# Outputs read 512 bytes at a time and K and V read 32 KB at a time in a grouped-query attention kernel

## The chip, the cores and the metric

The kernel runs on one core of a Trainium2 chip. The metric is the device time of one execution in microseconds (us), and lower is better. Differences between two kernels are judged on runs of both on the same chip.

## What is computed

Grouped-query attention with a softmax over all keys, in bfloat16. There are 16 batches, 32 query heads, 8 key/value heads, 16 query positions, 2048 key positions and a head size of 128.

```python
def reference(q, k, v):                     # q (16, 32, 16, 128), k and v (16, 8, 2048, 128)
    rep = Hq // Hkv                         # 4 query heads share one head of K and V
    k = jnp.repeat(k, rep, axis=1)
    v = jnp.repeat(v, rep, axis=1)
    scores = jnp.einsum("bhqd,bhkd->bhqk", q, k) * D ** -0.5
    p = _softmax(scores, axis=-1)
    return jnp.einsum("bhqk,bhkd->bhqd", p, v)
```

One (batch, key/value head) has 2048 x 128 values of K, 512 KB, as much of V, and 4 x 16 = 64 rows of queries. K and V together are 134.2 MB (millions of bytes), queries and outputs 2.1 MB each.

## The kernel before

**Pairs.** The 128 (batch, head) groups are worked on two at a time: 64 pairs, `NP`. The two groups' 64 query rows fill the 128 partitions. A pair needs one K tile and one V tile of 1 MB each (128 partitions of 8 KB) and makes one output tile of 128 rows of 256 bytes, 32 KB.

**The stages of a pair.** VectorE transposes the K tile in 32x32 blocks (L474). TensorE makes the scores in PSUM (L345). VectorE scales them into SBUF and takes each row's minimum (L494). GpSimd exchanges these between the two halves of the partitions (L216 to L224). ScalarE takes the exponentials (L542). TensorE transposes the probabilities (L363), ScalarE evicts them to SBUF (L553), and four pairs later (`PVLAG`) TensorE multiplies them with V (L415). ScalarE scales the product by the reciprocal row sum into an output tile (`norm`, L566). Every fourth pair a 128 KB tile of queries is spread and transposed for the next four pairs.

**Loads.** SyncE (SP) issues all K and V loads in one fixed order, K six pairs ahead of V (`VLAG`). K has `NK` = 8 buffers, and the load into a buffer waits until the transpose of its last tenant is done (L273). V has `NV` = 4 buffers, and a load waits until the product of the pair four before is done (L285). The helper `load` (L169) writes the descriptors' shape out by hand: the read side of a K or V tile is 64 runs of 16 KB, which are contiguous in DRAM, and the write side is 128 rows of 8 KB, so each run read is written into two partitions. The first two K tiles are ordinary copies of 128 rows of 8 KB (L276). The V tiles of the last eight pairs (from `P4` = 56) are loaded a head at a time, in reads of 8 KB that are written as two rows of 4 KB.

**Stores.** The outputs of the first `PH` = 48 pairs are stored one pair at a time by ScalarE's own DMA queue (`store`, L570): 128 reads of 256 bytes from SBUF, 128 writes of 256 bytes to DRAM. There are `NO` = 8 output buffers `Osb`, each with a semaphore `sem_o`; `norm` waits on it before it writes a buffer again. In a step, ScalarE runs `exp`, every second pair of four `queries`, `norm` of the pair four before, `evict`, and then issues that pair's store. The outputs of pairs 48 to 62 stay in the tile `Oh` and are stored at the end by SP (L300), and the last pair has a store of its own.

**Loops.** `steps` (L121) unrolls the first four steps, runs steps 4 to 51 in a hardware loop whose body has eight steps, and unrolls the rest. In the loop the pair's number is a register.

Of the kernel before, what the change touches and what calls it, by code (L numbers as in the profile page):

```python
# [12 lines left out]
NV = 4  # L13
NKT = 2
NPT = 4
NO = 8
NQ = 2
NR = 8
VLAG = 6
PVLAG = 4  # L20
# [5 lines left out]
def bass_standalone__gqa_softmax__sampling_kernel(  # L26
# [3 lines left out]
    v: bass.AP,  # L30
    out: bass.AP,
):

# [32 lines left out]
    Sneg = [sb(f"Sneg{i}", [128, Sk], F32) for i in range(2)]  # L68
    P = [sb(f"P{i}", [128, Sk // 2], F32) for i in range(2)]
    PT = [sb(f"PT{i}", [128, 8, 128], F32) for i in range(NPT)]  # L70
    Osb = [sb(f"O{i}", [128, 128], BF16) for i in range(NO)]
    Oh = sb("Oh", [128, sum(HELD), 128], BF16)

    own = sb("own", [128, NR, 4], F32)
# [43 lines left out]
    assert (HI - LO) % LOOP == 0 and HI <= P4 - 2  # L118


    def steps(eng, step, end):  # L121
        for p in range(LO):
            step(p, p)
        with eng.Fori(LO, HI, LOOP) as base:
            for i in range(LOOP):
                step(base + i, LO + i)
        for p in range(HI, end):
            step(p, p)


    def v_tile(p):
        return Kn[p % 4 + (NP - 8) % NK] if p >= NP - 4 else Vb[p % NV]

    def out_tile(p, i):
        return Oh[:, p - PH, :] if isinstance(p, int) and PH <= p < NP - 1 else Osb[i % NO][:, :]

    def stage_ap(u):
        return ST_ps[:, 512 * u:512 * (u + 1)]
# [27 lines left out]
        eng.dma_start(Qn[s][:, :, :].rearrange("a j d -> a (j d)"), src).then_inc(sem_q[s], 16)  # L166


    def load(eng, dst, src, x, n):  # L169
        ap = lambda t, dims: eng.lower_ap_dma(bass.AP(t.tensor, t.offset, dims))  # L170
        return eng.add_instruction(mybir.InstDMACopy(  # L171
            name=nc.get_next_instruction_name(), engine=eng.engine, mode="Copy", queue="qSPDynamicHW",
            ins=ap(src, [[n * x, 128 // n], [1, 1], [1, n * x]]), outs=ap(dst, [dst.ap[0], [1, 1], [1, x]])))

    lo, hi = slice(0, 64), slice(64, 128)

    with nc.Block() as block:
# [90 lines left out]
        @block.sync  # L268
        def _(sp):
            def load_k(p):  # L270
                s = p % NK
                if p >= NK:
                    sp.wait_ge(sem_kt, p - NK + 1)  # L273
                src = kf[128 * p:128 * (p + 1), :]
                if p < 2:
                    ins = sp.dma_start(Kn[s][:, :], src)  # L276
                else:
                    ins = load(sp, Kn[s][:, :], src, 4096, 2)
                ins.then_inc(sem_k[s], 16)

            def load_v(p):
                if p >= NP - 4:
                    sp.wait_ge(sem_kt, p - 3)
                elif p >= NV:
                    sp.wait_ge(sem_pv, p - NV + 1)  # L285
                dst = v_tile(p)[:, :]
                done = sem_vx[p - NP + 4] if NP - 4 <= p < NP - 1 else sem_v[p % NV]
                if p < P4:
                    load(sp, dst, vf[128 * p:128 * (p + 1), :], 4096, 2).then_inc(done, 16)
                    return  # L290
                dst = dst.rearrange("a (g x) -> a g x", g=2)
                src = vf4[:, 2 * p:2 * p + 2, :]
                if p < NP - 1:
                    for h in range(2):
                        load(sp, dst[:, h, :], src[:, h, :], 2048, 2).then_inc(done, 16)
                    return
                for n, x in enumerate((slice(0, 1536), slice(1536, 2048))):
                    sp.dma_start(dst[:, :, x], src[:, :, x]).then_inc(sem_vl[n], 16)

            def store_held(p, n):  # L300
                sp.wait_ge(sem_nm, p + n + 1)
                dst = of[128 * p:128 * (p + n), :].rearrange("(x r) d -> r x d", x=n)
                sp.dma_start(dst, Oh[:, p - PH:p - PH + n, :]).then_inc(sem_oh, 16)

            load_q(sp, 0, 0)
            for t in range(NP + VLAG):
                if t < NP:
                    load_k(t)
                for c in range(2, NQC):
                    if t == 4 * c - QLEAD:  # L310
                        if c == NQ:
                            sp.wait_ge(sem_q4d, 2)
                        sp.wait_ge(sem_q4, max(2, 4 * c - 6))
                        load(sp, Qn[c % NQ][:, :, :], qf[512 * c:512 * (c + 1), :], 512, 2).then_inc(sem_q[c % NQ], 16)
                if 0 <= t - VLAG < NP:
                    load_v(t - VLAG)
            p = PH
            for n in HELD:
                store_held(p, n)
                p += n  # L320
            sp.wait_ge(sem_oh, 16 * len(HELD))
            for s in range(NO):
                sp.wait_ge(sem_o[s], 16 * (PH // NO + 1 + (s == NO - 1)))

        @block.tensor
        def _(pe):
# [185 lines left out]
        @block.scalar  # L512
        def _(act):
            act.wait_ge(sem_id, 1)
            act.activation(warm[:, 1:2], warm[:, 0:1], ACT.Exp).then_inc(sem_nm, 1)

            with act.Fori(1, 2, 1) as c:
                load_q(act, c, 1)

            for s in range(NO):  # L520
                act.nop(nofuse=True).then_inc(sem_o[s], 16)


            def queries(c, b, base=0):
                act.wait_ge(sem_tq, base + 4 * c + 2 * b + 2)
                if c >= 2 and b == 0:
                    act.wait_ge(sem_qs, base + 4 * (c - 1))
                act.activation(  # L528
                    QT[c % 2][:, b, :].rearrange("p (a j) -> p a j", j=4),
                    q_stage_ap(c, b).rearrange("p (j a) -> p a j", j=4), ACT.Copy,  # L530
                ).then_inc(sem_evq, 2)

            def exp(p, i):
                act.wait_ge(sem_b, p + 1)
                if i >= 2:
                    act.wait_ge(sem_st[1], p - 1)
                order = "p (h t x) -> p h t x" if isinstance(p, int) and p >= P4 else "p (t h x) -> p h t x"
                to = P[i % 2][:, :].bitcast(BF16).rearrange(order, x=128, h=2)
                of_s = Sneg[i % 2][:, :].rearrange(order, x=128, h=2)
                s, t = i % NR, (i + 1) % NR  # L540
                for h in range(2):
                    ins = act.activation(  # L542
                        to[:, h], of_s[:, h], ACT.Exp,
                        bias=nbias[:, s, h:h + 1], scale=-1.0, accum_out=own[:, t, 2 + h:3 + h],
                    )
                ins.then_inc(sem_exp, 1)

            def evict(p, i):
                for h in range(2):
                    act.wait_ge(sem_st[h], p + 1)  # L550
                    if h == 0 and i >= NPT:
                        act.wait_ge(sem_pv, p - NPT + 1)
                    act.activation(  # L553
                        PT[i % NPT][:, 4 * h:4 * (h + 1), :].rearrange("p t q -> p (t q)"),
                        p_stage_ap(p, h), ACT.Copy,
                    ).then_inc(sem_ev[h], 1)

            def norm(p, i):
                s = i % NR
                act.wait_ge(sem_pv, p + 1)  # L560
                act.wait_ge(sem_rec, p + 1)
                if not isinstance(p, int) or p < PH:
                    act.wait_ge(sem_o[i % NO], 2 * (p - i) + 16 * (i // NO + 1))
                elif p == NP - 1:
                    act.wait_ge(sem_o[i % NO], 16 * (PH // NO + 1))
                act.activation(  # L566
                    out_tile(p, i), o_ap(p), ACT.Copy, scale=rrec[:, s:s + 1],
                ).then_inc(sem_nm, 1)

            def store(p, i):  # L570
                act.wait_ge(sem_nm, p + 2)
                rows = bass.ds(128 * p, 128)
                act.dma_start(of[rows, :], Osb[i % NO][:, :]).then_inc(sem_o[i % NO], 16)

            def step(p, i):
                exp(p, i)
                if i % 4 < 2 and (not isinstance(p, int) or p + 4 < NP):
                    queries(i // 4 + 1, i % 4, p - i)
                if i >= PVLAG:
                    norm(p - PVLAG, i - PVLAG)  # L580
                evict(p, i)
                if i >= PVLAG and (not isinstance(p, int) or p < PH + PVLAG):
                    store(p - PVLAG, i - PVLAG)

            for b in range(2):
                queries(0, b)
            steps(act, step, NP - 3)
            exp(NP - 3, NP - 3)
            norm(NP - 7, NP - 7)
            exp(NP - 2, NP - 2)  # L590
            evict(NP - 3, NP - 3)
            norm(NP - 6, NP - 6)
            exp(NP - 1, NP - 1)
            evict(NP - 2, NP - 2)
            norm(NP - 5, NP - 5)
            evict(NP - 1, NP - 1)
            for p in range(NP - 4, NP):
                norm(p, p)
            store(NP - 1, NP - 1)


# [26 lines left out]
```

## Time and profile before

| what | value |
|---|---|
| median of 3 runs | 335.8 us (335.75 to 336.75) |
| the profiled execution's own time | 335.8 us |
| its span, first to last instruction | 333.9 us |
| VectorE busy | 294.8 us, 88% |
| TensorE busy | 279.1 us, 84% |
| ScalarE busy | 258.8 us, 78% |
| GpSimd busy | 149.4 us, 45% |
| moved by DMA | 138.61 MB in 21854 packets, 415 GB/s over the span |

The profile counts the packets of the 16 DMA engines by what is read: one packet is one run that a transfer reads, and every transfer has 16 packets of 4 bytes besides, one for each engine, which count up its semaphore. The share of a queue is the time that its packets took, summed, divided by 16 times the length of the stretch. The queue q1 is SP's and q10 is ScalarE's.

### The profile page before, as it was taken

Reading aid. Unit: us, or ns where it says so; the run is one execution under the profiler, and the core shown is the slowest. Engines: PE = TensorE matmul, PEld = TensorE weight load, DVE = VectorE, ACT = ScalarE, POOL = GpSimd, SP = SyncE. Lnnn points to the kernel's source line nnn. Section 1 sums busy time; section 2 is a strip of 40 time slices with the busy share of each in tenths; the row PEclk is TensorE's granted clock in tenths of the full one; section 3 lists DMA queues with packets and bytes.
Section 4 is the critical chain, followed back from the end, with each engine's and each line's share of the span. In section 5 each row is a group of like instructions: output and inputs, shape, how many; then the busy total and the mean of one; then the engine's idle time right before and its main releaser. Section 6 shows DMA issues by size and latency. Waiting matters only on the chain.

```text
span 333.9 us, 16112 instructions
## 1 busy us (share of the span) xinstructions
PE 279.1 (84%) x6542; PEld 209.1 (63%) x6542; DVE 294.8 (88%) x354; ACT 258.8 (78%) x482; POOL 149.4 (45%) x488
## 2 busy tenths in 40 slices
PE   2557979999998989888897988979879798788786
PEld 1234757777776766666665766757657567667464
DVE  3999998999999989989898898998999989999930
ACT  3286887989897979779688787887878787886873
POOL 4444455353645544354445435354363453543330
PEclk9996999999999999999999999999999999999999
DMA  8999999999999999999999999999999999999997
GB/s 316 422 412 432 413 412 426 418 425 422 426 422 431 427 422 425 423 422 425 420 426 421 424 422 426 430 417 428 421 425 422 426 420 418 426 422 413 409 408 261
DMA packets 21854, 138.61 MB, mean 415 GB/s; under 512 B 11472, under 2 KB 11984, under 8 KB 13136
## 3 DMA queue, kind: packets, MB, share of 16 engines
q1 hardware_dynamic: 14640, 136.69, 97.7%
q10 hardware_dynamic: 7200, 1.74, 2.4%
q8 instruction: 8, 0.13, 0.2%
q14 instruction: 6, 0.05, 0.0%
HBM read 136.31 MB, written 2.10 MB: 415 GB/s over the span
## 4 chain that ended last, share of the span: by engine, by line
DMA 57%; PE 17%; DVE 16%; issue 7%; ACT 1%; SPq 1%; POOL 1%; DVEq 0%; POOLq 0%
DMA Vb<-in_v_dram 44%; PE O_ps L415 10%; DVE KT L474 9%; DMA Kn<-in_k_dram 8%; DVE Sneg L494 7%; DMA Kn<-in_v_dram 5%; PE ST_ps L363 3%; PE S_ps L345 3%; ACT P L542 1%; SPq L171 1%; PE ST_ps L378 1%; PE ST_ps L404 0%; POOL nbias L224 0%; SPq L276 0%; SPq L166 0%
## 5 line engine op out<-in xcount | busy, mean ns | idle before, releaser
L474 DVE STREAM_TRANSPOSE KT<-Kn 128x2048 f32<-128x2048 f32 x64 | 147.7, 2308 | 21.0 <-DMA Kn<-in_k_dram 20.9
L542 ACT ACTIVATE P<-Sneg,nbias 128x1024 bf16<-128x1024 f32 x128 | 146.0, 1142 | 15.1 <-POOL nbias L224 13.2
L494 DVE TENSOR_SCALAR_CACHE_REDUCE Sneg<-S_ps 128x1024 f32<-128x1024 f32 x128 | 149.9, 1206 | 3.0 <-PE S_ps L345 2.8
L415 PE MATMUL O_ps<-Vb,PT 64*64 64x128 bf16 x3584 | 111.1, 216 | 30.9 <-issue 26.8
L415 PEld LDWEIGHTS O_ps<-Vb,PT 64*64 64x64 bf16 x3584 | 102.9, 107 | 49.9 <-issue 49.9
L553 ACT ACTIVATE PT<-ST_ps 128x512 f32<-128x512 f32 x126 | 68.5, 594 | 15.7 <-PE ST_ps L363 15.0
L345 PE MATMUL S_ps<-KT,Qs 32*64 32x512 bf16 x2048 | 74.3, 399 | 6.0 <-DVE Sneg L494 3.9
L363 PE MATMUL ST_ps<-ident,P 128*128 128x128 f32 x504 | 69.7, 282 | 8.3 <-ACT P L542 8.3
L216 POOL COPY oth<-own 64x4 f32<-64x4 f32 (+1 forms) x65 | 11.9, 183 | 136.4 <-DVE Sneg L494 134.3
L363 PEld LDWEIGHTS ST_ps<-ident,P 128*128 128x128 f32 x504 | 54.7, 142 | 16.6 <-ACT P L542 10.9
L345 PEld LDWEIGHTS S_ps<-KT,Qs 32*64 32x64 bf16 x2048 | 27.6, 106 | 30.5 <-issue 17.1
L198 POOL COPY Qs<-QT 128x512 bf16<-128x512 bf16 x64 | 39.0, 610 | 12.1 <-POOL rowsum L231 6.0
L224 POOL TENSOR_SCALAR nbias<-own,oth 128x1 f32<-128x1 f32 x128 | 33.9, 280 | 10.6 <-POOL oth L219 9.0
L566 ACT ACTIVATE O<-O_ps,rrec 128x128 bf16<-128x128 f32 x48 | 17.5, 365 | 26.6 <-PE O_ps L415 26.5
L161 POOL COPY Q<-Qn 128x1024 bf16<-128x1024 bf16 x31 | 32.4, 1044 | 1.3 <-DMA Qn<-in_q_dram 1.3
L231 POOL TENSOR_TENSOR rowsum<-own,oth 64x1 f32<-64x1 f32 x128 | 23.8, 186 | 8.2
L378 PEld LDWEIGHTS ST_ps<-ident,Q 128*128 128x128 f32 x128 | 14.4, 148 | 18.3 <-issue 18.3
L378 PE MATMUL ST_ps<-ident,Q 128*128 128x128 f32 x128 | 22.1, 300 | 4.5 <-POOL Q L161 4.5
L542 ACT ACTIVATION_READ_ACCUMULATOR P<-Sneg,nbias 128x1 f32 x128 | 24.1, 188 | 0.0
L528 ACT ACTIVATE QT<-ST_ps 128x512 f32<-128x512 f32 x32 | 18.5, 578 | 3.7 <-PE ST_ps L378 3.7
L219 POOL COPY oth<-own 64x4 f32<-64x4 f32 (+1 forms) x65 | 11.8, 181 | 7.3
L566 ACT ACTIVATE Oh<-O_ps,rrec 128x128 bf16<-128x128 f32 x12 | 4.4, 367 | 9.6 <-PE O_ps L415 6.7
(30 smaller groups left out, 44.6 us busy)
## 6 DMA issues: line engine op xcount, KB each, us to landing
Kn<-in_k_dram SPq DMA_DIRECT2D x64, 1024.0 KB, 20.2
Vb<-in_v_dram SPq DMA_DIRECT2D x56, 1024.0 KB, 18.3
Vb<-in_v_dram SPq DMA_DIRECT2D x8, 512.0 KB, 15.6
Kn<-in_v_dram SPq DMA_DIRECT2D x6, 512.0 KB, 14.7
Qn<-in_q_dram SPq DMA_DIRECT2D x15, 128.0 KB, 20.0
out_dram<-O ACTq DMA_DIRECT2D x49, 32.0 KB, 8.9
Kn<-in_v_dram SPq DMA_DIRECT2D x1, 768.0 KB, 17.7
out_dram<-Oh SPq DMA_DIRECT2D x3, 128.0 KB, 15.8
```

Of the source, the lines that this page charges most:

```text
L161: return eng.tensor_copy(Q4[:, :, b, :, :], src.unsqueeze(2).to_broadcast([128, 4, 4, 64]))
L198: gp.tensor_copy(Qs[i % 2][:, :, :], QT[i // 4 % 2][:, :, 128 * x:128 * (x + 1)].bitcast(BF16)).then_inc(sem_qs, 1)
L224: ins = gp.tensor_scalar(nbias[:, s, h:h + 1], own[:, s, h:h + 1], oth[:, s, h:h + 1], None, op0=ALU.min)
L231: gp.tensor_tensor(rowsum[rows, t:t + 1], own[rows, s, 2 + h:3 + h], oth[rows, s, 2 + h:3 + h], op=ALU.add,).then_inc(sem_sum[h], 1)
L345: ins = pe.matmul(S_ps[64 * w:64 * (w + 1), 512 * r:512 * (r + 1)], qs[rows, b, f, 64 * h:64 * (h + 1)], kt[rows, w, b, f], start=(acc == ...
L363: ins = pe.transpose(dst[:, 128 * t:128 * (t + 1)], P[i % 2][:, 128 * x:128 * (x + 1)], ident4[:, :])
L378: ins = pe.transpose(dst[:, 128 * j:128 * (j + 1)], src[:, j, b, :], ident4[:, :])
L415: ins = pe.matmul(out[rows, :], pt[rows, w, t, e, :], vt[rows, x, :], start=(x == 0), stop=(x == 31),)
L474: ins = dve.transpose(dst, src)
L494: ins = dve.tensor_scalar(dst, src, -scale, None, op0=ALU.mult, op1=ALU.min, accum_out=own[:, i % NR, h:h + 1],)
L542: ins = act.activation(to[:, h], of_s[:, h], ACT.Exp, bias=nbias[:, s, h:h + 1], scale=-1.0, accum_out=own[:, t, 2 + h:3 + h],)
L553: act.activation(PT[i % NPT][:, 4 * h:4 * (h + 1), :].rearrange("p t q -> p (t q)"), p_stage_ap(p, h), ACT.Copy,).then_inc(sem_ev[h], 1)
```

## The change

The output buffers become four tiles of two pairs each (`NG` = 2, 512 bytes per partition). Once both pairs of such a tile are computed, two stores send it out, one step apart. Each takes half of the partitions, reads 64 rows of 512 bytes, and writes each as two rows of 256 bytes, one in each pair's output. There is still one store for each of the 48 pairs. With f the first pair of a tile, the stores are issued in steps f + 5 and f + 6, where the stores of f and f + 1 were issued in steps f + 4 and f + 5. `norm` waits for a buffer only at the first pair of a tile, and `store` waits for the computed values only at the first half. The store is now built by hand, as the loads are, by a helper `copy` that `load` calls too.

In `load`, the read side of each K tile from the third on, and of the V tiles of the first 56 pairs, becomes 32 runs of 32 KB instead of 64 of 16 KB. The write side stays 128 rows of 8 KB, so each run is written into four partitions. V tiles of the last eight pairs, the queries and the stores from `Oh` stay as they are.

ScalarE's hardware loop runs from step 5 to step 44 instead of step 4 to step 51, so more of its steps are unrolled. The other engines' loops stay.

```diff
-NO = 8
+NG = 2
+NO = 8 // NG
...
-    Osb = [sb(f"O{i}", [128, 128], BF16) for i in range(NO)]
+    Osb = [sb(f"O{i}", [128, NG, 128], BF16) for i in range(NO)]
...
-    def steps(eng, step, end):
+    def steps(eng, step, end, first=LO, last=HI):
...
+    SLAG = NG - 1 + PVLAG
+    SHI = SLAG + (PH + PVLAG - SLAG) // LOOP * LOOP
+    placed = lambda n: 16 * NG * (n + 1)
...
+    def copy(eng, dst, dst_dims, src, src_dims):
+
+        limit = [] if isinstance(dst.offset, int) else [mybir.RegisterAccess(
+            regref="Activation_bcreg1_lo", dtype=I32, ant_hi_reg="Activation_bcreg1_hi")]
+        ap = lambda t, dims: eng.lower_ap_dma(bass.AP(t.tensor, t.offset, dims)) + limit
+        return eng.add_instruction(mybir.InstDMACopy(
+            name=nc.get_next_instruction_name(), engine=eng.engine, mode="Copy",
+            queue="qSPDynamicHW" if eng.engine == mybir.EngineType.SP else "qActDynamicHW",
+            ins=ap(src, src_dims), outs=ap(dst, dst_dims)))
...
     def load(eng, dst, src, x, n):
...
+        return copy(eng, dst, [dst.ap[0], [1, 1], [1, x]], src, [[n * x, 128 // n], [1, 1], [1, n * x]])
...
-                    ins = load(sp, Kn[s][:, :], src, 4096, 2)
+                    ins = load(sp, Kn[s][:, :], src, 4096, 4)
...
-                    load(sp, dst, vf[128 * p:128 * (p + 1), :], 4096, 2).then_inc(done, 16)
+                    load(sp, dst, vf[128 * p:128 * (p + 1), :], 4096, 4).then_inc(done, 16)
...
             def norm(p, i):
...
-                    act.wait_ge(sem_o[i % NO], 2 * (p - i) + 16 * (i // NO + 1))
+                    if i % NG == 0:
+                        act.wait_ge(sem_o[i // NG % NO], 2 * NG * (p - i) + placed(i // LOOP))
...
-            def store(p, i):
-                act.wait_ge(sem_nm, p + 2)
-                rows = bass.ds(128 * p, 128)
-                act.dma_start(of[rows, :], Osb[i % NO][:, :]).then_inc(sem_o[i % NO], 16)
+            def store(p, i, x):
+                if x == 0:
+                    act.wait_ge(sem_nm, p + NG + 1)
+                s, n = i // NG % NO, 128 // NG
+                dst = of[bass.ds(128 * p + n * x, n), :]
+                src = Osb[s][n * x:n * (x + 1), :, :]
+                copy(
+                    act, dst, [[128, n], [128 * 128, NG], [1, 128]], src, [src.ap[0], [1, 1], [1, NG * 128]],
+                ).then_inc(sem_o[s], 16)
...
-                if i >= PVLAG and (not isinstance(p, int) or p < PH + PVLAG):
-                    store(p - PVLAG, i - PVLAG)
+                if i >= SLAG:
+                    x = (i - SLAG) % NG
+                    if not isinstance(p, int) or p - SLAG - x < PH:
+                        store(p - SLAG - x, i - SLAG - x, x)
...
-            steps(act, step, NP - 3)
+            steps(act, step, NP - 3, SLAG, SHI)
```

## The prediction

> **What bounds the kernel now.** I read the page's slices first.
>
> ```profile
> span 333.9 us, 16112 instructions
> ...
> DMA  8999999999999999999999999999999999999997
> ...
> q1 hardware_dynamic: 14640, 136.69, 97.7%
> q10 hardware_dynamic: 7200, 1.74, 2.4%
> ```
>
> The 16 DMA engines are busy in every slice, and the packets' times add up to the span (97.7% loads and the stores from `Oh`, 2.4% ScalarE's stores). Next, the chain of waits in order of time:
>
> ```profile
> 129.63 18.27 DMA Vb<-in_v_dram
> 147.91 0.14 issue
> 148.04 1.99 PE O_ps L415 x64
> 150.03 0.02 issue
> 150.05 18.27 DMA Vb<-in_v_dram
> ```
>
> From 110 to 270 us the chain is: a V load lands 18.27 us after its issue, the product runs 1.99 us, the buffer is free, the next V load is issued. One round is 150.05 - 129.63 = 20.42 us and covers four pairs, 5.1 us a pair. The 18.27 us are mostly queueing: 18.27 us at 423 GB/s are 7.7 MB, seven tiles. So a round shortens only if the engines get through its packets sooner. Can the rest keep up? The windows table (after the bounds and the length: PE, PEld, DVE, ACT and POOL busy, clock, DMA share, GB/s):
>
> ```profile
> 57.00:97.00 40.00, 38.81 (x957) 29.73 (x956) 40.00 (x50) 35.85 (x69) 20.08 (x66) 1.00 1.02 424
> 109.85:272.46 162.61, 138.72 (x3393) 106.30 (x3394) 148.15 (x179) 130.20 (x242) 74.33 (x240) 1.00 1.01 423
> ```
>
> From 57 to 97 us the computation, late from the start, works off landed tiles: nine pairs in 40 us, 4.4 us each, VectorE without a gap. Later it idles at 5.1 us a pair. Computation becomes the bound only after 0.6 us a pair have gone from the transfers; this change is worth less. So I cost it in packet time on one DMA engine, and that goes one to one into the span until the last V tile lands at 330.35 us.
>
> **What a packet costs.** I looked for stretches of the DMA queues that hold one kind of packet: the first K tiles (8 KB read, one 8 KB row written) at 6.50 to 6.62 us, K at 8.60 to 8.80 (16 KB, two rows), queries at 2.00 to 2.23 (1 KB), the last store alone at 332.80 to 333.10 (128 of 256 bytes, 16 of 4 bytes), late V at 320.29 to 320.90 (8 KB, two rows of 4 KB):
>
> ```profile
> q1 hardware_dynamic: 11, 0.09, 177.3%
> ...
> q1 hardware_dynamic: 11, 0.18, 210.0%
> ...
> q1 hardware_dynamic: 42, 0.04, 52.2%
> ...
> q10 hardware_dynamic: 144, 0.03, 50.1%
> ...
> q1 hardware_dynamic: 28, 0.23, 92.9%
> ```
>
> Share times 16 times length, over the count, is the time of one packet. 8 KB: 1.773 x 16 x 120 / 11 = 309.5 ns. 16 KB: 610.9 ns. 1 KB: 45.7 ns. Last store: 2405 ns in all; with 9 ns for each 4-byte packet (my estimate, half of a store's) the 256-byte ones take (2405 - 144) / 128 = 17.7 ns. Two 8 KB packets cost 2 x 309.5 - 610.9 = 8.1 ns more than one of 16 KB with the same two rows, so this much belongs to the read packet and not to the row.
>
> But neighbours overlap. From 109.85 to 272.46 us:
>
> ```profile
> DMA packets 10355, 68.85 MB, mean 423 GB/s; under 512 B 5769, under 2 KB 5769, under 8 KB 6281
> ...
> q1 hardware_dynamic: 5730, 67.79, 98.4%
> q10 hardware_dynamic: 4624, 1.05, 3.0%
> ```
>
> The shares sum to 101.4%. Engines cannot be over 100% busy, so 1.4% of 16 x 162.61 us, 36.4 us, is overlap: 3.5 ns a packet. A removed packet therefore saves its fixed part less 3.5 ns.
>
> **K and V reads.** 62 K tiles and 56 V tiles go from 64 packets to 32: 118 x 32 / 16 = 236 packets fewer on each engine. Saved: 236 x (8.1 - 3.5) = 1.09 us. Bounds: 236 x 8.1 = 1.9 us gained if the overlap goes with the packets; a loss is not excluded, since no packet of before writes four rows (third rival).
>
> **Stores.** 48 x 64 / 16 = 192 packets fewer on each engine. No 512-byte read is in the trace; between 17.7 ns (256) and 45.7 ns (1 KB) a straight line gives 17.7 + 28.0 / 3 = 27.0 ns. Two of before cost 35.4 ns, so 8.4 ns go, less 3.5: 192 x 4.9 = 0.94 us. Bounds: 1.6 us without the overlap, nothing if the 256-byte writes set the pace (second rival), and a loss as above.
>
> The Trainium skill, "DMA: Bandwidth & Descriptors", section "Why small descriptors are slow (HBM only)", states about 3 cycles of fixed overhead per packet, 11 cycles for 256 bytes. At the 850 MHz that the same page gives for the fabric (section "Where 436 GB/s comes from") this is 3.5 ns, an estimate, and the two terms would be 428 x 3.5 = 1.5 us instead of 2.0. The rows above give 4.6 and 4.9, and I keep them.
>
> **What is moved, and what covers it.** Stores leave a step later. A buffer's second store is issued six steps after its first pair's step, and `norm` needs the buffer twelve steps after it, 30 us later at 5.1 us; stores land in 8.9 us:
>
> ```profile
> out_dram<-O ACTq DMA_DIRECT2D x49, 32.0 KB, 8.9
> ```
>
> A store's packets take turns with K and V packets twice as long, but an engine has four instead of eight, so the landing stays near 9 us. Without this cover (over 30 us) `norm` would hold back `evict` and the next `exp`. No wait is added; two go in every second step.
>
> Issuing a store occupies ScalarE 0.34 us (L573) plus 0.08 us of register work. Hand-built copies on SP take 0.47 to 0.60 us (L171) where the ordinary K copy takes 0.42 (L276), so I expect 0.05 us more, bounds 0 to 0.26. Behind it stand `exp` and `evict`. ScalarE has (162.61 - 130.20) / 32 = 1.0 us a pair outside its work, 0.42 of it issue and register work, so 0.6 us covers this. In 57 to 97 us it is nearly full (35.85 + 9 x 0.42 = 39.6 of 40), but the shortest landing of a V load from 36 us on is 9.2 us, so the queue holds about four tiles: even 14 pairs x 0.26 = 3.6 us late leave it filled. Uncovered, this would be 14 x 0.05 = 0.7 us. Eight more unrolled steps on ScalarE mean about one more instruction fetch, nothing against 138 MB. SP issues as many loads as before and mostly waits for products. In the tail, late V, `Oh` and everything after 330.35 us stay.
>
> **Sum.** 333.9 - 1.09 - 0.94 = 331.9 us of span. The profiled execution took 335.8 us, 1.9 us around the span, and is equal to the median of the runs shown. Forecast: 335.8 - 2.0 = 333.8 us.
>
> **Rivals.** (1) *The overlap goes with the packets:* 1.9 + 1.6 = 3.5 us, 332.3 us. Against it: the 101.4% hold over stretches with and without small packets.
> (2) *The stores gain nothing*, because each pair's row is still a write of 256 bytes, and no row shows a store whose reads and writes differ. Then only K and V count: 335.8 - 1.1 = 334.7. For it: nothing in the trace separates read from write in a store. Against it: reads of one size into more rows do not pay where it can be seen (8 and 16 KB). If the K and V term fails too (the descriptors are cut again, or four rows cost what was saved), the time is 335.8.
> The same page, section "Specifications", speaks for (2): under 512 bytes a DMA does a read-modify-write. No run here shows it.
> (3) *Slower: changing rows inside a packet costs.* Late V, two 4 KB rows, takes 0.929 x 16 x 610 / 28 = 323.8 ns, 14.3 more than 8 KB in one row. If that is the price of a row change inside a packet, a 32 KB packet has three where two of 16 KB had two: 236 x (14.3 - 4.6) = 2.3 us lost, and for the stores 192 x (14.3 - 4.9) = 1.8 lost: 339.9 us, 338.1 with K and V alone. It decides from 4.6 ns a change on. Against it: the 16 KB packet has one change and is cheaper than two packets without any.
>
> **Numbers.** Forecast 0.48 (own range 333.2 to 334.4); (1) 0.09; (2) 0.20; nothing at all 0.11; (3) 0.12. What a measurement here can tell from no change is about 0.3%, 1.0 us. (2) lies at that edge, so half of it counts as faster: 0.48 + 0.09 + 0.10 = 0.67 faster, 0.10 + 0.11 = 0.21 same, 0.12 slower. The range reaches from (1) to 336.8, the highest run of before, which is the end of no gain; only most of (3) is outside.
>
> **What would show it.** Right: 3776 packets fewer in q1 and 3072 fewer in q10; 1214 ns per 32 KB packet; q10's share down from 2.4 to about 1.9%; a round of 20.42 - 16 x 4.6 - 16 x 4.9 ns = 20.27 us in the chain. (2) is right if a 512-byte packet takes 32 ns or more (two of before, less one overlap), (3) if a 32 KB one takes over 1218 (the same). Wrong altogether: a chain that leaves the V loads between 110 and 270 us, a landing of stores beyond 30 us, or a share of DMA below 1.00 there.

## The result: 0.43% slower, and the profile after

The changed kernel takes 337.48 us (median of 20 executions) against 335.77 us before: a ratio of the means of 1.0043, 95% interval 1.003 to 1.0055. The forecast was 333.8 us. The executions before lie close together (most between 335.6 and 336.1 us); those after spread from 336.04 to 339.84 us, and the profiled one took 337.47 us. A second series of the same changed kernel, below, came out at 336.09 us.

The page of the changed kernel (queue, packets, MB, share of 16 engines):

```profile
span 335.7 us, 16085 instructions
...
DMA  8999999999999999999999999999999999999997
...
q1 hardware_dynamic: 10864, 136.69, 97.4%
q10 hardware_dynamic: 4128, 1.74, 1.9%
...
out_dram<-O ACTq DMA_DIRECT2D x49, 32.0 KB, 9.2
```

The change does what it says: 14640 - 10864 = 3776 packets fewer in q1, 7200 - 4128 = 3072 fewer in q10, whose share falls to 1.9%. The stores land in 9.2 us (8.9 before). But q1's share hardly moves. Its chain of waits:

```profile
151.26 18.28 DMA Vb<-in_v_dram
169.54 0.14 issue
169.68 1.99 PE O_ps L433 x64
171.68 18.23 DMA Vb<-in_v_dram
```

The chain still runs through the V loads. From the product at 149.25 us to the one at 271.61 us a round of four pairs takes 20.39 us, against 20.41 before (148.04 to 270.49). Forecast was 20.27. So the steady part gained next to nothing. And the start lost. The windows table from 45 to 65 us (bounds and length, five busy times, clock, DMA share, GB/s), first before, then after:

```profile
45.00:65.00 20.00, 18.38 (x459) 14.20 (x454) 18.81 (x23) 16.64 (x33) 9.29 (x30) 1.00 1.02 421
```

```profile
45.00:65.00 20.00, 16.64 (x414) 12.98 (x417) 17.57 (x22) 15.66 (x30) 8.91 (x29) 1.00 0.98 396
```

Before, the DMA engines move 421 GB/s here, after only 396: (421 - 396) / 421 x 20 us = 1.2 us of transfers are missing, and nothing makes up for them later. The engines ran dry while the computation was late. TensorE's timeline between 36 and 56 us, the lines with an idle time of "issue" (start, duration, instruction; in brackets the idle time ahead of it), before:

```profile
44.10 1.81 PE L415 MATMUL O_ps<-Vb,PT 64*64 64x128 bf16 x57 [0.64 <-issue]
...
50.34 1.19 PE L415 MATMUL O_ps<-Vb,PT 64*64 64x128 bf16 x36 [1.46 <-issue]
```

and after:

```profile
39.80 0.42 PE L363 MATMUL S_ps<-KT,Qs 32*64 32x512 bf16 x8 [0.75 <-issue]
...
47.19 1.80 PE L433 MATMUL O_ps<-Vb,PT 64*64 64x128 bf16 x57 [2.07 <-issue]
...
53.25 1.19 PE L433 MATMUL O_ps<-Vb,PT 64*64 64x128 bf16 x36 [1.29 <-issue]
```

These gaps cut through the middle of a product, the one at 39.80 us through scores. The profile shows nothing that TensorE waits for there. They come in the first pass through its loop, beside instruction fetches of 16 KB (queue q8). They add up to 4.1 us instead of 2.1. The product ends later, V's buffer is free later, and the next V load is issued later: the third after 36 us at 49.02 us instead of 45.94. Loads then find a shorter queue (V loads issued from 36 to 60 us, issue to landing, before and after):

```profile
DMA to landing us min/median/max: 9.2/9.7/10.1
```

```profile
DMA to landing us min/median/max: 6.5/7.8/9.0
```

ScalarE may add to it: a store's issue takes longer than the 0.34 us of before.

```profile
L184 ACTq DMA_DIRECT2D out_dram<-O x48: 541/563/681, 44.0 to 274.6; - x48
```

That is 0.22 us more per pair (0.05 were forecast, 0.26 was the bound).

So there are two questions: why fewer packets bring nothing in the steady part, and what makes the start late. The theories at this point, by the names that the expectations use: A, TensorE's instruction fetches queue behind longer packets; B, ScalarE's longer store delays the computation; C, 32 KB packets written in four rows are slower as such.

### The profile page after: what moved, and what is told of

It is laid out like the page before. It is cut to its first block, busy times and chain, and to the rows that moved or that the text cites. A ratio compares the mean times of both kernels' runs of the same rounds, so it can differ in the third digit from the quotient of the medians.

```text
span 335.7 us, 16085 instructions
## 1 busy us (share of the span) xinstructions
PE 280.8 (84%) x6542; PEld 210.2 (63%) x6542; DVE 294.9 (88%) x354; ACT 258.2 (77%) x482; POOL 150.2 (45%) x488
## 3 DMA queue, kind: packets, MB, share of 16 engines
q1 hardware_dynamic: 10864, 136.69, 97.4%
q10 hardware_dynamic: 4128, 1.74, 1.9%
## 4 chain that ended last, share of the span: by engine, by line
DMA 51%; PE 25%; issue 8%; ACT 8%; DVE 3%; ACTq 2%; POOL 1%; SPq 1%; POOLq 0%; DVEq 0%
DMA Vb<-in_v_dram 43%; PE O_ps L433 11%; DMA Kn<-in_k_dram 8%; PE ST_ps L381 6%; ACT P L560 6%; PE S_ps L363 5%; DVE Sneg L512 3%; PE ST_ps L396 2%; ACTq L184 1%; ACT PT L571 1%; DVE KT L492 1%; POOL nbias L242 1%; PE ST_ps L443 1%; ACT QT L546 0%; PE ST_ps L422 0%
## 5 line engine op out<-in xcount | busy, mean ns | idle before, releaser
L381 PE MATMUL ST_ps<-ident,P 128*128 128x128 f32 x504 | 71.1, 286 | 8.7 <-ACT P L560 8.6
L381 PEld LDWEIGHTS ST_ps<-ident,P 128*128 128x128 f32 x504 | 55.9, 145 | 17.0 <-ACT P L560 11.4
```

Of the source, the lines that this page charges most:

```text
L381: ins = pe.transpose(dst[:, 128 * t:128 * (t + 1)], P[i % 2][:, 128 * x:128 * (x + 1)], ident4[:, :])
```

## The experiments

"Low" is the lowest execution. "Late" counts those over 0.6 us above it, wherever they lost the time. The round is that of four pairs, the mean of six, from the starts of products in the chain between 147 and 277 us. The packet is the mean K or V packet between 130 and 270 us (130 to 200 for the loads alone), worked out from the queue's share as shown below; since the engines are busy all the time, it says where a round's time lies, not why.

| run | reads of K, V | stores | median us | low | late | round us | packet ns |
|---|---|---|---|---|---|---|---|
| before | 16 KB | 256 B | 335.8 | 335.6 | 33 of 157 | 20.41 | 615 |
| changed | 32 KB | 512 B, halves | 337.48 | 336.04 | 13 of 20 | 20.39 | 1232 |
| changed, again | 32 KB | 512 B, halves | 336.09 | 335.91 | 3 of 10 | 20.40 | |
| loads only | 32 KB | 256 B | 338.71 | 337.84 | stores back up | | 1227 |
| stores only | 16 KB | 512 B, halves | 336.74 | 336.52 | 3 of 12 | 20.45 | 619 |
| loads of 8 KB | 8 KB | 256 B | 337.23 | 336.76 | 6 of 12 | 20.49 | 311 |
| late 32 KB | 16, from pair 24 32 KB | 512 B, halves | 336.34 | 336.03 | 2 of 12 | 20.41 | |
| full store | 16 KB | 512 B, all partitions | 336.90 | 336.65 | 2 of 12 | 20.45 | |
| full store, 32 KB | 32 KB | 512 B, all partitions | 336.97 | 336.27 | 6 of 12 | 20.41 | |
| halves of 256 B | 16 KB | 256 B, halves | 339.73 | 338.56 | ScalarE bound | | |
| early 32 KB | 32, from pair 24 16 KB | 512 B, halves | 337.33 | 336.39 | 6 of 12 | | |
| rows of 4 KB | 16 KB in 4 rows | 256 B | 342.67 | 342.66 | 0 of 5 | 20.87 | 630 |

**One part alone, the opposite step, and 32 KB late.** The loads' edit, the last number being the partitions per read, for K and V alike (1 for reads of 8 KB; `4 if p >= 24 else 2` for late 32 KB):

```diff
-                    ins = load(sp, Kn[s][:, :], src, 4096, 2)
+                    ins = load(sp, Kn[s][:, :], src, 4096, 4)
```

> Only the K and V reads of 32 KB; stores as before. Theory A (TensorE's instruction fetches queue behind longer packets in the first 60 us, the product comes late, V loads are issued late, the DMA engines run dry): 'issue' gaps of TensorE between 36 and 56 us sum to about 4 us as in the changed kernel (2.1 us before), the engines run dry for some 0.5 to 1 us, and the time is 336.5 to 338, as much slower than before as the whole change. Theory B (ScalarE's longer store, 0.56 us instead of 0.34, makes the computation late): nothing is slower, 335.5 to 336. The round of four pairs from 150 to 270 us: 20.4 us if fewer reads bring nothing there, 20.35 if the 4.6 ns per packet of the prediction hold.

> Only the new stores; K and V in reads of 16 KB as before. Theory A: no loss at the start, gaps of TensorE about 2.1 us as before, and the time is between 334.8 and 335.9 (the prediction's store term is 0.94 us at most). Theory B: the loss is here, 336.5 to 338, with the engines running dry between 50 and 63 us. The round from 150 to 270 us: 20.34 us by the prediction's 4.9 ns a packet, 20.42 if stores gain nothing.

> Stores as before; K and V tiles in reads of 8 KB, each written to one row: 64 packets more per engine and round of four pairs, 472 more in the whole kernel... the opposite step of the change. If a read packet has its own price of 4.6 ns (the prediction): the round is 20.42 + 32 x 4.6 ns = 20.57 us and the kernel 2.2 us slower, 338. If reads cost nothing in the steady part (bytes or written rows set the pace): the round stays 20.42 and the time 335.8. Theory A adds: TensorE's gaps at 36 to 56 us shrink below 2.1 us, since a fetch waits for shorter packets, with no gain in time, because the engines do not run dry in the kernel before.

> The whole change, but K and V tiles of the first 24 pairs are read in 16 KB. Theory A: the start is as in the run with the new stores alone, so the loss of about 1 us between 50 and 80 us is gone; what is left is what 32 KB reads do in the steady part and at the end (the last tile landed 0.8 us later than the start explains): 335.2 to 336.4. Theory C (32 KB packets written in four rows are slower as such): the loss stays in proportion to the 32 KB tiles, 74 of 118, over 336.5.

(With 8 KB an engine has 32 packets more per round, not 64; 472 in all is right.)

*Loads only* was slower by more than the whole change (1.0076, interval 1.0045 to 1.0108), but not by any of the theories. ScalarE's waits, and the landing of the stores:

```profile
ACT O L566 <- DMA out_dram<-O: 31.7, 11, 3.9
```

```profile
DMA to landing us min/median/max: 1.5/24.5/51.0
```

`norm` waits 31.7 us for output buffers: stores take up to 51 us. The two queues take turns packet by packet: from 130 to 200 us of this run each gets 1630 through.

```profile
q1 hardware_dynamic: 1630, 29.26, 98.4%
q10 hardware_dynamic: 1630, 0.37, 2.5%
```

In the time of a pair an engine has 4 packets of K and V, 1 of queries and 2.25 of semaphores, some 7 turns, and a store of before needs 8 + 1. It backs up until all eight buffers are out. The changed store needs 4 + 1 and fits. The two halves of the change belong together.

*Stores only* costs 0.9 us where 0.94 us were to be gained. That is within theory B's range, but the start did not run dry (420 GB/s from 45 to 65 us), so it is not B's loss. The queues from 130 to 270 us, before, then with the changed stores alone:

```profile
DMA packets 8921, 59.36 MB, mean 424 GB/s; under 512 B 4961, under 2 KB 4961, under 8 KB 5409
...
q1 hardware_dynamic: 4950, 58.45, 98.5%
q10 hardware_dynamic: 3970, 0.91, 3.0%
```

```profile
DMA packets 7170, 59.10 MB, mean 422 GB/s; under 512 B 1434, under 2 KB 3226, under 8 KB 3674
...
q1 hardware_dynamic: 4928, 58.17, 98.7%
q10 hardware_dynamic: 2240, 0.92, 2.4%
```

Before, q1 has 4961 - 3970 = 991 semaphore packets (9 ns), 5409 - 4961 = 448 of queries (2 KB, some 84 ns, an estimate between the 1 KB and the 8 KB packet of the prediction) and 3511 of K and V. These took 0.985 x 16 x 140 us - 38 - 9 = 2159 us, 615 ns each. With the changed stores it is 3494 packets in 2164 us, 619 ns. The store packets themselves cost what was forecast: (0.024 x 2240 us - 448 x 9 ns) / 1792 = 28 ns, instead of two of 18. But a round has two K or V packets to each of them, and each of those is 4.2 ns longer. The 8.4 ns that a store packet saves are back in its neighbours, and the overlap of 3.5 ns per removed packet is lost besides: 16 x 3.5 = 0.06 us a round, where 0.04 are seen. Over the 12 rounds that have stores 0.04 us are 0.5 of the 0.9 us. The profiles show where some of the rest is: this run is 0.44 us behind at the product at 270.93 us (270.49 before) and 0.8 at the end, with TensorE standing 0.60 us instead of 0.30 ahead of the product at 296.51 us (295.72 before). What that has to do with the stores, which are done by then, is open.

*Reads of 8 KB* are slower by 336.92 - 335.77 = 1.15 us (medians of the executions that are not late), 2.4 ns for each of the 472 added packets. *Late 32 KB*, against the stores alone, is 336.74 - 336.34 = 0.40 us faster with 144 packets fewer on each engine, 2.8 ns each, and the start of its profiled execution loses nothing (420 GB/s from 45 to 65 us). So a read packet of K or V has a net price, but about half of the forecast's 4.6 ns. Theory C falls. Theory B alone does not bring the 1.2 us: the changed stores were there in both runs whose start was full. Nor did theory A's expectation for reads of 8 KB come true: TensorE's gaps are 1.01 + 1.57 = 2.6 us there, not below 2.1.

**What about the stores? All partitions, halves of the old store, and 32 KB only early.** First one store of 128 partitions at every second step, then the kernel before with each store in two halves:

```diff
-                if i >= SLAG:
-                    x = (i - SLAG) % NG
...
+                if i >= SLAG and (i - SLAG) % NG == 0:
+                    if not isinstance(p, int) or p - SLAG < PH:
+                        store(p - SLAG, i - SLAG)
```

```diff
-                rows = bass.ds(128 * p, 128)
-                act.dma_start(of[rows, :], Osb[i % NO][:, :]).then_inc(sem_o[i % NO], 16)
+                for x in range(2):
+                    rows = bass.ds(128 * p + 64 * x, 64)
+                    act.dma_start(of[rows, :], Osb[i % NO][64 * x:64 * (x + 1), :]).then_inc(sem_o[i % NO], 16)
```

> K and V in reads of 16 KB; the two pairs' outputs leave in one store of all 128 partitions (128 reads of 512 bytes, two rows of 256 bytes each) every second step. In the run with the changed stores over 16 KB reads each K and V packet took 619.4 ns in the steady part, 4.2 more than before, and that ate the 8.4 ns saved per pair of store packets. Theory H (the store that reads only half of the partitions makes the 16 engines read through a part of SBUF's ports and slows the loads): here the K and V packets are back at 615, the round is 20.34 us or less, the time 334.5 to 335.5. Theory W (512-byte reads written as two rows, or reads as long as that, slow the loads wherever they come from): 619 again, a round of 20.45, 336.5 to 337.

> The same store of all partitions, with K and V in reads of 32 KB throughout. Theory H and the start: the steady part is faster than the kernel before (round 20.30 to 20.35), but the start loses as in the changed kernel, where the engines ran dry between 50 and 63 us: 335 to 337, with a spread of runs over 1 us. Theory W: as the changed kernel, 336.5 to 338.

> The kernel before, but each pair's store is cut into two stores of 64 partitions (64 reads of 256 bytes each): as many data packets as before, 16 semaphore packets and one more issue on ScalarE a pair. Theory H: the K and V packets of 16 KB rise from 615.2 to 618 or more in the steady part and the round gets longer than the four more semaphore packets per engine (4 x 5.5 ns = 0.02 us) explain: 20.5 us or more, 336.5 or more. Theory W: packets stay at 615, round 20.44, time 335.8 to 336.5.

> The whole change, but reads of 32 KB only for the first 24 pairs' tiles, 16 KB from then on (the opposite of the run with late 32 KB reads). If the reads of 32 KB cost at the start and gain later: slower than with the changed stores alone (336.74) by some 1 us, 337.5 to 338.5, with a spread of runs over 1 us, and TensorE's gaps between 36 and 56 us longer than there (2.45 us). If the start loss of the changed kernel was chance of the profiled execution: 336.5 to 336.9.

Theory H, that a store of half of the partitions slows the loads, falls. With stores of all partitions the time (336.90) and the round (20.45) are those of the changed stores, not those of before; it is the 512-byte read written as two rows that brings nothing. ScalarE's issues are not the reason either: there are 24 of 0.55 us in this run instead of 48 of 0.56. The halves of 256 bytes, whose K and V packets stay at 614 ns, end at 339.73 us for another reason, on ScalarE (who waited for whom, us, times, longest):

```profile
ACT P L542 <- issue: 40.3, 48, 1.6
```

After each pair of issues the next exponential starts 0.84 us late, and ScalarE becomes the bound. This is what ScalarE's store would cost without cover: the price of an issue was small only because one fits in. With 32 KB only early the kernel takes 337.33 us, just under the expected 337.5 to 338.5, and TensorE's gaps are 2.6 us, hardly more than the 2.45 with the stores alone.

**Written rows.**

```diff
-    def load(eng, dst, src, x, n):
+    def load(eng, dst, src, x, n, r=1):
...
-            ins=ap(src, [[n * x, 128 // n], [1, 1], [1, n * x]]), outs=ap(dst, [dst.ap[0], [1, 1], [1, x]])))
+            ins=ap(src, [[n * x, 128 // n], [1, 1], [1, n * x]]),
+            outs=ap(dst, [dst.ap[0], [x // r, r], [1, x // r]])))
...
-                    ins = load(sp, Kn[s][:, :], src, 4096, 2)
+                    ins = load(sp, Kn[s][:, :], src, 4096, 2, 2)
```

> The kernel before, with the K and V reads of 16 KB written as four rows of 4 KB instead of two of 8 KB: as many read packets, 64 more written rows per engine and round of four pairs. Theory R (the written rows set the pace, reads are hidden behind them; so merging reads saves little and merging the stores' reads nothing): each more row costs some 3 to 5 ns, the round rises from 20.41 to between 20.6 and 20.75 us, the K and V packets from 615 to 621 ns or more, the time to 338.5 to 341. If the price belongs to the read packet, as the prediction had it: round 20.41, packets 615, time 335.8.

The queues from 130 to 270 us in this run:

```profile
DMA packets 8735, 58.08 MB, mean 415 GB/s; under 512 B 4852, under 2 KB 4852, under 8 KB 5300
...
q1 hardware_dynamic: 4854, 57.18, 98.6%
q10 hardware_dynamic: 3880, 0.88, 3.0%
```

The reads are the same, the written rows twice as many, and the kernel takes 342.67 us, 2% more (1.0203, interval 1.019 to 1.0216). A packet takes (2209 - 47) / 3434 = 630 ns, some 14.5 more for two more rows. 118 tiles x 128 / 16 = 944 rows more on each engine and 6.8 us: 7.2 ns a row, where 3 to 5 were expected, against 2.4 to 2.8 ns for a read packet of K or V. For the loads most of the price is on the side of the written rows, and the change leaves their number as it was. That it is so for the rows of the stores in DRAM fits their result, but no run changes their number.

**The start.** The changed kernel with 16 KB only for the 15 tiles in flight while TensorE fetches its loop, the inverse, 32 KB in the first 24 pairs with the old stores, and a second profile of the changed kernel. The edit for K (V's has `3 <= p <= 9`):

```diff
-                    ins = load(sp, Kn[s][:, :], src, 4096, 4)
+                    ins = load(sp, Kn[s][:, :], src, 4096, 2 if 9 <= p <= 16 else 4)
```

> The whole change, but 16 KB reads for the 15 tiles (K of pairs 9 to 16, V of pairs 3 to 9) that are in flight from about 33 to 58 us, when TensorE fetches its loop for the first time. Theory A (these fetches wait behind 32 KB packets): the loss at the start is gone as in the run with 16 KB for the first 24 pairs: median 336.0 to 336.4, few runs above 337. If 32 KB reads cost at the start for another reason: median 337 or more and half of the runs above 337, as in the changed kernel.

> The inverse: 32 KB reads for these 15 tiles alone, 16 KB everywhere else, with the changed stores. Theory A: the loss at the start is here: median 337 to 338, spread over 1 us, half of the runs above 337. Otherwise as with the changed stores alone, 336.5 to 336.9.

> The kernel before with its stores of 256 bytes, and 32 KB reads only for the first 24 pairs' tiles. If 32 KB reads alone make the start late: median 336.5 to 337.5, a third of the runs or more above 337, the engines dry between 50 and 80 us. If the loss needs the changed store as well (0.56 us of ScalarE instead of 0.34 in each step of the start): as before, 335.6 to 336.0. Stores of 256 bytes take turns with 32 KB packets and may back up by the end of the 24 pairs (nine packets a pair, some seven turns), which would show as landings above 20 us but not as a wait, since the 16 KB packets come before the eight buffers are used up.

> The changed kernel once more, for a second profile. If the loss at the start goes with TensorE's gaps: an execution near 336.2 shows gaps of about 2.5 us in sum between 36 and 56 us and full engines, one near 338 shows over 3.5 us and dry engines.

With 16 KB for these tiles the changed kernel takes 336.36 us (1.0017, interval 1.0008 to 1.0025), 2 of 12 late, as theory A has it. But the changed kernel as it is took 336.09 us in its second series, 3 of 10 late, so this run does not show that the edit took the loss away. The inverse does not bring it back: 336.79 us, 2 of 6 late, against its expectation. With the old stores, 5 of 12 are late (median 335.71, low 335.49), so the changed store is not needed for late executions. The second profile of the changed kernel caught an execution of 336.07 us; its TensorE gaps, a product and the windows line, and the same product in the first profile, 1.2 us later:

```profile
46.13 1.80 PE L433 MATMUL O_ps<-Vb,PT 64*64 64x128 bf16 x57 [1.84 <-issue]
...
52.47 1.19 PE L433 MATMUL O_ps<-Vb,PT 64*64 64x128 bf16 x36 [1.57 <-issue]
...
148.07 1.99 PE O_ps L433 x64
...
45.00:65.00 20.00, 17.31 (x425) 13.30 (x427) 17.45 (x23) 15.36 (x31) 8.89 (x30) 1.00 0.99 411
```

```profile
149.25 1.99 PE O_ps L433 x64
```

The gaps add up to 3.4 us, where 2.5 were expected, and the engines keep nearly full. The two executions differ by 335.7 - 334.2 = 1.5 us of span, and 149.25 - 148.07 = 1.2 us of it are there by this product: for the same kernel, most of the difference is the start.

How often does it happen? In the profiles of all runs the engines ran dry at the start in three: the changed kernel, 32 KB early, and 32 KB with full stores. From 45 to 80 us they moved 409, 409 and 411 GB/s, all others 418 to 426 (but 414 with rows of 4 KB, whose rate later is 415). All three have a single gap over 2 us (2.07, 2.03, 2.39), no other profile has one over 1.84. In the last two the granted TensorE clock was also 0.91 from 45 to 65 us (1.00 in the changed kernel), but so it was in the profile of 32 KB for K alone, at 335.3 us one of the fastest. Of all executions with 32 KB reads at the start 40 of 78 are late, of those with 16 KB there 33 of 157 of the kernel before and 11 of 70 of the other kernels (the run bound by ScalarE left out). The share differs from series to series, but in each of the four that have both it is higher with 32 KB than in the kernel before: 13 of 20 against 2 of 20, 12 of 24 against 10 of 31, 8 of 22 against 3 of 23, and 7 of 12 against 4 of 17.

Two things stand against a plain story. Of reads of 8 KB 6 of 12 are late. And a late execution need not be a late start: with 32 KB and full stores the profiled execution (337.43 us, 1.2 above the lowest) is 0.3 us behind the kernel before at the product at 148.34 us and at the one at 270.79 us, but 335.5 - 333.9 = 1.6 us at the end.

The fetches themselves are in the trace (queue q8): in all profiles those from 35 to 52 us take 1.1 to 1.2 us each, whatever the reads, and a gap ends 1.2 to 1.5 us after one. So a longer gap belongs to a fetch that began later, not to one that took longer, and no trace shows when it was asked for. That longer packets make late executions more frequent is what the counts show; that the wait of a fetch behind a packet is the way it happens stays open.

**Versions from the findings.** The old stores issued by SP on the loads' queue, with late 32 KB reads; the old stores with 32 KB for K alone; and that from pair 20 on only. For the first, in SP's loop behind `load_v`, with ScalarE's store dropped:

```diff
+                if 0 <= t - 11 < PH:
+                    store(t - 11)
```

> A version built from the findings: outputs stored pair by pair with reads of 256 bytes as before, but issued by SP on the queue of the loads, so that they take no turns with them and ScalarE issues nothing in the loop; K and V in 32 KB from pair 24 on, 16 KB ahead of it. If a 32 KB read saves the 2 to 3 ns net per removed packet that the runs with 8 and 32 KB reads show in the steady part, and ScalarE's freed time keeps the start full: 335.2 to 335.6. If SP's issues delay the loads behind them: 335.8 to 337.

> The kernel before with its stores of 256 bytes, and 32 KB reads for the K tiles alone (all from the third on), 16 KB for V. An engine has 2 + 4 + 1 packets of K, V and queries and 2.25 of semaphores a pair, 9.25 turns for the 9 packets of a store, so the stores should not back up for good (landings below 40 us). If removed read packets save 4.6 ns each (the prediction), the round of four pairs is 20.41 - 8 x 4.6 ns = 20.37 us and the kernel 0.57 us faster than before, 335.2; if with the old stores they save nothing (2 x 615.2 against 1226.7 ns is 3.7, as much as the overlap that is lost), 20.41 and 335.8. If the stores do back up: waits of ScalarE for a store and 337 or more.

> A version built from the findings: the kernel before with its stores, V in 16 KB throughout, K in 32 KB from pair 20 on and 16 KB ahead of it. The run with 32 KB for all K tiles had executions near 335.3 (0.4 under the kernel before) and others above 336.3. If the latter come from 32 KB reads at the start: nearly all executions at 335.2 to 335.6 here, the median 0.2 to 0.5 us under the kernel before. If not: a third or more above 336.3 again and a median of 335.8 or more.

Stores on SP's queue: 337.41 us, where 335.2 to 337 were expected, with a round of 20.54 us (chain of waits of this run):

```profile
148.41 1.99 PE O_ps L421 x64
...
271.62 1.99 PE O_ps L421 x64
```

(271.62 - 148.41) / 6 = 20.54. The round is 0.13 us longer than before, although from pair 24 on it has 16 read packets fewer: the same 256-byte packets cost more in line with the loads than when they take turns with them from another queue. 32 KB for K alone has the lowest execution of all, 335.29 us, but 7 of 12 are late and the median is 336.49 (1.0007, interval 0.9987 to 1.0028). Only from pair 20 on: 335.61 against 335.79 us, 2 of 12 late, a round of 20.38 us; the ratio of 0.9996 (0.9973 to 1.002) does not tell it from the kernel before. No version clearly beats it.

## Why the prediction was wrong

**The bound** was right: the chain stayed on the V loads from 149 to 292 us, and the time there went one to one with what the DMA engines got through. The count of packets, the 27 ns of a 512-byte packet, the landing of the stores and ScalarE's bound were right too.

**The K and V term** had the right sign and twice the size. 4.6 ns per removed packet came from 8.1 ns at 6 to 9 us, where the packets are the shortest (309.5 and 610.9 ns). In the steady part it is 2 x 311 - 615 = 7 ns from 8 to 16 KB, less the overlap, and 2.4 to 2.8 ns measured from the times. 236 x 2.6 = 0.6 us instead of 1.09. The mark for the third rival (a 32 KB packet over 1218 ns) was taken from the same quiet stretch and so misled: 1232 ns were measured, but two of 16 KB take 1230 in the steady part, and 1238 with the changed stores.

**The store term is the step that failed:** "192 x 4.9 = 0.94 us" saved. The store packets took what was said, 28 ns instead of two of 18, but the K and V packets beside them got longer by the same sum, 619 ns instead of 615. The 256-byte rows that the stores write are as many as before, which may be why; no run shows it for stores. Measured: 336.74 - 335.82 = 0.9 us lost, 0.5 of it in the rounds with stores. My second rival came nearest (the 256-byte writes set the pace), but priced it at nothing, not at a loss, and its mark (32 ns or more for a 512-byte packet) was not met. I took each queue's packets by themselves, although they share an engine. The third rival's 338.1 us lies nearest to the measured time, but by chance: it has the K and V reads lose 2.3 us, and they gained.

These two make 335.8 + 0.9 - 0.6 = 336.1 us, which is where the changed kernel's executions lie when they are not late (median 336.22; 336.07 in the second series).

**What no step or rival named** is the rest, 337.48 - 336.1 = 1.4 us in the median of the first series: the late executions, in the profiled one a late start. In the second series this rest is nothing in the median, so how much of it a measurement finds is chance in part. I counted the landing of 9.2 us as cover for 3.6 us of ScalarE's lateness and never asked what else the computation waits for there. TensorE's gaps of 0.64 and 1.46 us stood in the trace of before. What makes them longer stays open.

The Trainium skill, "DMA: Bandwidth & Descriptors", section "Why small descriptors are slow (HBM only)", with 3 cycles a packet, an estimate of 3.5 ns, was nearer to the K and V packets' 2.4 to 2.8 ns than my rows. Its rule of 512 bytes, section "Specifications", pointed the right way for the stores; that read-modify-write is the reason no run shows.

## What to carry to other kernels

Price a DMA packet where it will run, beside the traffic it shares an engine with, and count the written rows apart from the reads: here a row of K or V cost 7.2 ns and a read packet 2.4 to 2.8. Before packets of one queue are made longer, count the turns that are left to the queues that alternate with them, small stores above all. And where a buffer's cover is thinnest (here 36 to 65 us), look for every wait, not only for those of the engine that the change touches.

## What was not expected of the hardware

Moving the stores to SP's queue made the kernel slower, 337.41 against 335.88 us, with the same store packets and fewer packets of K and V. The Trainium skill, "DMA: Bandwidth & Descriptors", section "Issuing engines are not separate DMA queues", says that issuing from several engines only saves the sequencer's time, as all run on the same DMA engines. Here the measurement differs: small packets that alternate with long ones from another queue were cheaper by at least 0.13 / 32 us = 4 ns each than in line with them.
